# Seven products in tiles 4 to 6 and casts one tile ahead: a fused attention and feed-forward kernel on one core

## The chip, the cores and the metric

The kernel runs on one core of one Trainium2 chip. The metric is device microseconds of one execution; lower is better. TensorE (PE) multiplies, VectorE (DVE) and ScalarE (ACT) work on tiles elementwise, GpSimd (POOL) casts and issues some DMAs, SyncE (SP) issues most DMAs. All engines run their own queues and wait for each other by semaphores.

## The reference

```python
# q, k, v: (8, 8, 576, 64) float32; w_in: (512, 2048); w_out: (2048, 512)
scores = matmul(q, k^T) / sqrt(64), kept where abs(i - j) <= 32
attn   = softmax(scores)
x      = matmul(attn, v), heads side by side: (8 * 576 = 4608 tokens, 512)
h      = x @ w_in
g      = gelu_tanh(h)
out    = g @ w_out          # (4608, 512) float32
```

## The kernel before

**Tiles and batches.** The 4608 tokens are nine tiles of 512, t = 0 to 8. Tile t has a first stage, the input projection `x @ w_in` with its gelu, and a second stage, the output projection with its stores. Attention is computed per batch (b = 0 to 7, 576 tokens each) one tile ahead: tile t carries the attention of batch b = t + 1 between the products of its second stage. The result goes into `xT`, a ring of 1536 tokens from which the later tiles read.

**First stage.** `ffn_in(t, n)` makes one of 16 blocks of 128 hidden columns with four matmuls 512 wide (L577). `gelu` moves it from PSUM to `gTs[t]` on ACT (L585). After every fourth block `sums` (L694) adds and subtracts blocks on DVE into S1 to S4, four instructions for each of four groups. The first three blocks of a tile are begun at the end of the tile before (`begun`). In tiles 7 and 8 another path is taken: `in_x` (L614) makes four differences of the tokens, `in_mixed` (L632) walks the list `MIX`, and `in_product` (L616) computes two groups, A and B, of four blocks each as seven products of four matmuls 256 wide (L629) instead of 16 matmuls 512 wide. The weight sums for this come from `in_w` (L604), made earlier, in the second stages of tiles 3, 4 (group B) and 6 (group A).

**Second stage.** `ffn_out(t, i)`, i = 0 to 111, issues seven products of 16 matmuls 256 wide (L751), after the same scheme. Two PSUM banks take turns: products 0, 2, 4, 6 use one, products 1, 3, 5 the other. After each product a DVE instruction takes the bank's value (L762 to L789), and the product after the next may write to that bank only when this is done. So product 5, at i = 80, waits for L771, the DVE instruction behind product 3.

**Where attention stands.** `PLAN` says in front of which i a piece of attention is issued: "s" scores (L468) and exp (L481), "m" mask (L490, DVE), "v" sums and weighted values (L495, L505) with their inverse on ACT (L530, L531), "x" the scaled result into `xT` (L540, L546, DVE). The number is the head pair; 4 and -1 are the last 24 tokens of this and of the previous batch. `PLAN_1` is the same for tile 1.

**How the inputs come in.** At the start of tile t's second stage `load_qk(b + 1)` puts on SP's queue one DMA of 1 MB for q, four of 256 KB for k (one for each 128 keys, all heads) and the tails (the last 64 positions). At the start of the next tile, `open_and_turn` and `turn_keys` cast them to 16 bit on DVE, four instructions for q (L410) and four for k (L419); each k cast reads the same two heads of all four k DMAs. After them SP issues transposing DMAs into `QTs` and `KTs`, and `turn_tails` does the same for the tails (`KLs`). V of the next batch comes by POOL's queue at i = 4, after a copy named `after` that waits for `KLs`. SP and DVE take their queues in the program's order.

Of the kernel before, what the change touches and what calls it, by code (L numbers as in the profile page):

```python
# [36 lines left out]
def cut(b):  # L37
# [8 lines left out]
PLAN = {7: "s0@0 s1@1 v-1", 16: "m0 m1 x-1", 33: "s2@0 v0@1 v1", 36: "m2", 44: "x0", 50: "x1",  # L46
        62: "s3@0 s4@1 v2", 66: "m3", 80: "x2", 84: "m4", 91: "v3", 112: "x3"}
# [14 lines left out]
MIX = ("3 g3 A0 s0A B0 s0B 12 g12 A2 B2 cA00 cB00 A1 s1A gA00 A4 B1 s1B gB00 B4 t0 u0 13 g13 A3 s3A B3 s3B 14 g14 "  # L62
       "cA11 cB11 A5 gA10 B5 gB10 gA11 gB11 A6 B6 cA01 cB01 15 gA01 gB01 t1 t2 g15 t3 u1 u2 u3").split()
UNITS = {"A": 1, "B": 2}

PLAN_1 = {12: "s0@0 s1@1 s2", 16: "m0 m1", 36: "m2", 56: "s-1@0 v0@1 v1", 62: "m-1 x0", 64: "x1",
          78: "s3@0 v2 v-1@1", 79: "m3", 88: "x2", 91: "x-1", 97: "v3 s4@1", 112: "x3 m4"}
# [5 lines left out]

RING = 1536
# [4 lines left out]
def kernel(  # L79
# [29 lines left out]
    rawp = ctx.enter_context(tc.tile_pool(name="rawp", bufs=2))  # L109
# [27 lines left out]
    def load_early(b):  # L137


        qr = rawp.tile([128, H, 256], FP32, name="qr")  # L140
        kr = rawp.tile([128, H, 256], FP32, name="kr")
        raws[b] = [qr, kr, None]

        def qk(h0, queues=(nc.sync, nc.sync)):
            for src, dst, queue in zip((q, k), (qr, kr), queues):
                queue.dma_start(
                    dst[:, h0:h0 + 2, :],
                    src[b, h0:h0 + 2, 0:512, :].rearrange("h (p j) d -> p h (j d)", j=4))

        def vs(*cs):  # L150
            if len(raws[b]) < 4:
                raws[b].append(stage.tile([128, 4, H, 64], FP32, name="vr", tag="stage"))
                raws[b].append(tailp.tile([128, 4, 64], FP32, name="vt", tag="vt"))
            for c in cs:
                if c == 4:
                    for x in range(2):
                        nc.sync.dma_start(raws[b][4][64 * x:64 * x + 64, :, :],
                                          v[b, 4 * x:4 * x + 4, 512:S, :].rearrange("h p d -> p h d"))
                else:
                    nc.sync.dma_start(raws[b][3][:, c, :, :],  # L160
                                      v[b, :, 128 * c:128 * c + 128, :].rearrange("h p d -> p h d"))

        def tails(which="qk"):
            if raws[b][2] is None:
                raws[b][2] = tailp.tile([128, H, 64], FP32, name="tr", tag="tr")
            tr = raws[b][2]
            if b == 0:
                for i, src in enumerate((q, k)):
                    for x in range(2 if "qk"[i] in which else 0):
                        nc.sync.dma_start(tr[64 * x:64 * x + 64, 4 * i:4 * i + 4, :],  # L170
                                          src[b, 4 * x:4 * x + 4, 512:576, :].rearrange("h s d -> s h d"))
                return
            for h in (0, 4):
                for x, src in enumerate((q, k)):
                    nc.sync.dma_start(tr[64 * x:64 * x + 64, h:h + 4, :],
                                      src[b, h:h + 4, 512:576, :].rearrange("h s d -> s h d"))

        return qk, tails, vs

    def load_qk(b):  # L180


        if b == 3:
            qr = raws[3]
        else:
            qr = rawp.tile([128, H, 256], FP32, name="qr")
            load_q(b, qr)
        kr = rawp.tile([128, 4, H, 64], FP32, name="kr")
        if b > 3:
            qt = tailp.tile([16, H, 256], FP32, name="qt", tag="vt")  # L190
            kt = tailp.tile([64, H, 64], FP32, name="kt", tag="tr")
            raws[b] = (qr, kr, qt, kt)
        else:
            raws[b] = [qr, kr, tailp.tile([128, H, 64], FP32, name="tr", tag="tr"), None]
        for c in range(4):
            nc.sync.dma_start(kr[:, c, :, :],
                              k[b, :, 128 * c:128 * c + 128, :].rearrange("h p d -> p h d"))
        load_tails(b, nc.sync)
        if b == 3:
            load_vr(3)  # L200
# [4 lines left out]
    def load_tails(b, queue):  # L205
        if b > 3:
            queue.dma_start(raws[b][2], q[b, :, 512:576, :].rearrange("h (p j) d -> p h (j d)", j=4))
            queue.dma_start(raws[b][3], k[b, :, 512:576, :].rearrange("h p d -> p h d"))
        else:
            queue.dma_start(raws[b][2][0:64, :, :], q[b, :, 512:576, :].rearrange("h s d -> s h d"))  # L210
            queue.dma_start(raws[b][2][64:128, :, :], k[b, :, 512:576, :].rearrange("h s d -> s h d"))
# [190 lines left out]
    def load_vr(b):  # L402
        vr = vrs[b] = rawp.tile([128, 4, H, 64], FP32, name="qr")
        for c in range(4):
            nc.sync.dma_start(vr[:, c, :, :],
                              v[b, :, 128 * c:128 * c + 128, :].rearrange("h p d -> p h d"))

    def turn_queries(b, src, dst, p0, p1):
        for pr in range(NPAIR):
            nc.vector.tensor_copy(  # L410
                dst[:, pr, :, :, :].rearrange("p j h d -> p h j d"),
                src[:, 2 * pr:2 * pr + 2, :].rearrange("p h (j d) -> p h j d", j=4))
        nc.sync.dma_start_transpose(QTs[b].rearrange("d r j p -> d (r j) p")[:, :, p0:p1],
                                    dst.rearrange("p r j h d -> p (r j h d)"))

    def turn_keys(b):
        k16, kr = halfs[b][1], raws[b][1]
        for pr in range(NPAIR):
# [6 lines left out]
    def turn_tails(b):  # L425
        qt, kt = raws[b][2:4]
        qt16 = hp.tile([16, NPAIR, 4, 2, 64], FP16, name="qt16", tag="qt16")
        kt16 = hp.tile([64, NPAIR, 2, 64], FP16, name="kt16", tag="t16")
        turn_queries(b, qt, qt16, 128, 144)
        nc.vector.tensor_copy(kt16.rearrange("p r h d -> p (r h d)"), kt.rearrange("p h d -> p (h d)"))  # L430
        nc.sync.dma_start_transpose(
            KLs[b % 2], kt16.rearrange("p r h d -> p (r h d)"))

    def open_and_turn(b):
        cast_open(b)
        turn_queries(b, raws[b][0], halfs[b][0], 0, 128)
# [154 lines left out]
    def in_w(eng, unit, *which):  # L591
# [3 lines left out]
        if (unit, "s") not in mixed:  # L595
            halves = [(rawp if unit == "A" else yp).tile([128, 2, 2, 2, 128], FP16, name="wc" + unit + str(x),
                                                         tag=("qr", "kr")[x] if unit == "A" else "yo") for x in range(2)]
            mixed[unit, "s"] = [half[:, x] for half in halves for x in range(2)]
# [7 lines left out]
    def in_x(t):  # L606
# [3 lines left out]
        xc = hp.tile([128, 4, 2, 256], FP16, name="xc", tag="q16" if t % 2 else "k16")  # L610
# [5 lines left out]
    def in_product(unit, n):  # L616
        a, w, new = WINO[n]
        if n == 0:
            phs[unit, "a"] = psO.tile([128, 512], FP32, name="pu", tag="O") if unit == "A" else bank(1)
        elif n in (2, 4):  # L620
            which = "b" if n == 2 else "c"
            if unit == "A":
# [9 lines left out]
    def in_mixed(t):  # L632
        if "A" not in mixed:
            mixed["A"] = rawp.tile([128, 3, 512], FP32, name="sa", tag="qr")
            mixed["B"] = rawp.tile([128, 3, 512], FP32, name="sb", tag="kr")

        place = {"00": (0, "b"), "01": (1, "c"), "11": (2, "c")}
        for step in MIX:
            kind, rest = step[0], step[1:]
            if kind in UNITS:  # L640
                in_product(kind, int(rest))
# [16 lines left out]
            elif kind in "tu":  # L658
                sums(t, int(rest), slice(0, 2) if kind == "t" else slice(2, 4))
# [72 lines left out]
    def ffn_out(t, i):  # L732

        n, blk, f = i // 16, i // 8 % 2, i % 8
        if n == 1 and t >= NT - 2:
            blk, f = divmod(i % 16, 6) if i % 16 < 12 else (i // 2 % 2, 6 + i % 2)
# [28 lines left out]
        elif n == 2:  # L765
            nc.vector.tensor_copy(C11, py)
            if end:
# [162 lines left out]
    for t in range(NT):  # L930
        b = t + 1
        att = b < B
        if t:
# [8 lines left out]
            elif att:  # L942
                if b > 3:
                    open_and_turn(b)
                turn_keys(b)
                if b > 3:
                    turn_tails(b)
# [4 lines left out]
            for fc in range(begun, NF if t < NT - 2 else 0):  # L952
                ffn_in(t, fc)
                if t == 1 and fc == 3:
# [4 lines left out]
                    raws[3] = rawp.tile([128, H, 256], FP32, name="qr")  # L959
                    load_q(3, raws[3])  # L960
                    combine(4, nc.vector)
                if t == 1 and 6 <= fc < 10:
                    cast_v(2, fc - 6)
                if t == 1 and fc == 8:
                    trans_tails(1, psO.tile([128, 8, 128], FP16, name="pt", tag="O"))
# [9 lines left out]
                if t > 1 and fc == 8 and att:  # L975
                    pair_v(b, nc.vector.tensor_copy)
        plan = PLAN_0 if not t else PLAN_1 if t == 1 else PLAN if att else {40: "v-1", 66: "x-1"} if t == B - 1 else {}
# [6 lines left out]
        if t and b + 1 < B:  # L984
            load_qk(b + 1)
        ods = {}
        for i in range(113 if t else 65):
# [8 lines left out]
            for act in plan.get(i, "").split():  # L996
# [47 lines left out]
                elif kind == "m":  # L1044
                    mask(*group(g))
                elif kind == "v":
# [11 lines left out]
            if t in (3, 4) and i == 52:  # L1058
                in_w(nc.vector, "B", *((1, 2) if t == 3 else (3, 4)))
# [12 lines left out]
            elif t and i < 112:  # L1072
                ffn_out(t, i)
# [36 lines left out]
```

## Time and profile before

| | |
|---|---|
| runs | 296.6, 297.36, 1631.62 us; median 297.36 |
| profiled execution | 296.65 us |
| its span, first to last instruction | 294.6 us |
| PE busy | 285.9 us, 97% |
| DVE busy | 212.4 us, 72% |
| ACT busy | 196.5 us, 67% |
| first stage of tile 4 (176.00 to 190.38) | 14.38 us, DVE busy 11.16 |
| its second stage (190.38 to 206.50) | 16.12 us, DVE busy 11.23 |

The profile is one execution. "Span" counts from the first to the last instruction on the core; the execution's own time is 2.05 us more. The third run is far from the other two and is not used. A matmul's shown end is a model, so its start-to-start distance tells its rate: 0.216 us for 512 columns, 0.109 us for 256 columns.

### The profile page before, as it was taken

Reading aid. Unit: us, or ns where it says so; the run is one execution under the profiler, and the core shown is the slowest. Engines: PE = TensorE matmul, PEld = TensorE weight load, DVE = VectorE, ACT = ScalarE, POOL = GpSimd, SP = SyncE. Lnnn points to the kernel's source line nnn. Section 1 sums busy time; section 2 is a strip of 40 time slices with the busy share of each in tenths; the row PEclk is TensorE's granted clock in tenths of the full one; section 3 lists DMA queues with packets and bytes.
Section 4 is the critical chain, followed back from the end, with each engine's and each line's share of the span. In section 5 each row is a group of like instructions: output and inputs, shape, how many; then the busy total and the mean of one; then the engine's idle time right before and its main releaser. Section 6 shows DMA issues by size and latency. Waiting matters only on the chain.

```text
span 294.6 us, 7286 instructions
## 1 busy us (share of the span) xinstructions
PE 285.9 (97%) x2945; PEld 192.7 (65%) x2945; DVE 212.4 (72%) x467; ACT 196.5 (67%) x315; POOL 88.8 (30%) x143
## 2 busy tenths in 40 slices
PE   8889999999999999999999999999999999999993
PEld 3535545547765687568755885588558867887783
DVE  4755477998897667858796878686957877865762
ACT  5965877777677874787667776796669558706800
POOL 4445335004228713205250615050800050025000
PEclk9999999999999999999999999999999999999998
DMA  7999998999999998999999999899691040004013
GB/s 229 275 380 396 359 305 196 254 186 203 248 229 202 251 202 188 113 139 245 162 212 94 246 157 191 116 245 154 117 190 7 0 118 28 2 26 120 0 47 99
DMA packets 114392, 51.02 MB, mean 173 GB/s; under 512 B 98471, under 2 KB 110247, under 8 KB 114102
## 3 DMA queue, kind: packets, MB, share of 16 engines
q1 hardware_dynamic: 89460, 38.67, 62.4%
q0 software_dynamic: 23776, 10.83, 23.4%
q10 hardware_dynamic: 1122, 1.06, 1.1%
q8 instruction: 23, 0.38, 0.6%
q14 instruction: 11, 0.09, 0.1%
HBM read 36.70 MB, written 9.44 MB: 157 GB/s over the span
## 4 chain that ended last, share of the span: by engine, by line
PE 85%; DVE 5%; DMA 5%; issue 1%; SPq 1%; ACT 1%; POOL 0%; DVEq 0%
PE mm L751 32%; PE ph L577 17%; PE mm L577 16%; PE ps_s L468 4%; PE pu L629 3%; DMA kr<-in_k_dram 3%; PE mm L723 2%; DMA wst<-in_moe_w_in_dram 2%; PE py L723 2%; PE ps_d L495 2%; PE ps_o L505 2%; DVE t L684 2%; DVE s L694 1%; PE mm L629 1%; PE ps_od L495 1%; PE ps_od L505 1%
## 5 line engine op out<-in xcount | busy, mean ns | idle before, releaser
L577 PEld LDWEIGHTS <-w_in 128*128 128x128 f16 x512 | 57.4, 113 | 49.8 <-POOL w_in L250 1.5
L577 PE MATMUL ph<-xT,w_in 128*128 128x512 f16 x256 | 64.5, 379 | 0.6 <-POOL w_in L250 0.6
L577 PE MATMUL mm<-xT,w_in 128*128 128x512 f16 x256 | 64.1, 379 | 0.0
L585 ACT ACTIVATE gT<-mm 128x512 f16<-128x512 f32 x60 | 35.6, 598 | 33.3 <-PE mm L577 32.7
L713 POOL DMA_DIRECT2D out_dram<-y x55 | 32.8, 605 | 82.4 <-DVE y L780 75.3
L751 PEld LDWEIGHTS <-s 128*128 128x128 f16 x512 | 49.3, 98 | 7.1 <-DVE s L694 0.6
L751 PE MATMUL mm<-t,s 128*128 128x256 f16 x376 | 45.2, 273 | 0.2 <-DVE y L764 0.2
L694 DVE TENSOR_TENSOR s<-gT 128x512 f16<-128x512 f16 x64 | 27.5, 430 | 19.1 <-ACT gT L585 18.9
L751 PEld LDWEIGHTS <-gT 128*128 128x128 f16 x384 | 36.2, 98 | 6.4
L585 ACT ACTIVATE gT<-ph 128x512 f16<-128x512 f32 x58 | 32.4, 604 | 10.9 <-PE ph L577 10.9
L481 ACT ACTIVATE pe<-ps_s 128x960 f16<-128x960 f32 (+1 forms) x31 | 29.5, 975 | 13.2 <-PE ps_s L468 13.1
L751 PE MATMUL mm<-w_out,gT 128*128 128x256 f16 x256 | 32.6, 273 | 0.0
L104 ACT ACT_TABLE_LOAD x18 | 23.1, 1283 | 2.2 <-issue 1.9
L530 ACT ACTIVATE lt<-ps_d 128x480 f32<-128x480 f32 (+2 forms) x28 | 15.6, 556 | 10.4 <-PE ps_d L495 6.9
L531 ACT ACTIVATE lt<-lt 128x480 f32<-128x480 f32 (+3 forms) x36 | 21.1, 585 | 1.1
L490 DVE TENSOR_TENSOR pe<-pe,band 128x960 f16<-128x960 f16 x28 | 18.5, 680 | 2.0 <-ACT pe L481 1.9
L505 PEld LDWEIGHTS <-V 128*64 128x64 f16 x520 | 13.7, 111 | 5.5 <-DVE V L226 1.5
L751 PE MATMUL mm<-t,gT 128*128 128x256 f16 x128 | 16.1, 273 | 0.0
L694 DVE TENSOR_TENSOR s<-s,gT 128x512 f16<-128x512 f16 x32 | 14.0, 436 | 1.1
L216 POOL DMA_DIRECT2D V<-in_v_dram x16 | 14.3, 908 | 1.1 <-PE ps_s L468 0.4
L751 PE MATMUL mm<-w_out,s 128*128 128x256 f16 x120 | 14.6, 273 | 0.0
L540 DVE TENSOR_TENSOR xT<-ps_o,lt 128x480 f16<-128x480 f32 (+5 forms) x26 | 13.4, 535 | 1.6 <-PE ps_o L505 1.6
(149 smaller groups left out, 390.3 us busy)
## 6 DMA issues: line engine op xcount, KB each, us to landing
kr<-in_k_dram SPq DMA_DIRECT2D x31, 256.0 KB, 10.2
qr<-in_q_dram SPq DMA_DIRECT2D x6, 1024.0 KB, 5.9
wst<-in_moe_w_in_dram SPq DMA_DIRECT2D x8, 512.0 KB, 6.6
wst<-in_moe_w_out_dram SPq DMA_DIRECT2D x2, 1024.0 KB, 10.5
wst<-in_moe_w_out_dram SPq DMA_DIRECT2D x4, 512.0 KB, 7.4
qr<-in_v_dram SPq DMA_DIRECT2D x8, 256.0 KB, 6.5
V<-in_v_dram POOLq DMA_DIRECT2D x16, 128.0 KB, 8.5
qr<-in_q_dram SPq DMA_DIRECT2D x7, 256.0 KB, 7.3
```

Of the source, the lines that this page charges most:

```text
L104: nc.scalar.add_instruction(mybir.InstLoadActFuncSet(name=nc.get_next_instruction_name(), act_func_set_id=which, ins=[], outs=[]))
L216: nc.gpsimd.dma_start(V[:, c, :, :], v[b, :, 128 * c:128 * c + 128, :].rearrange("h p d -> p h d"))
L481: nc.scalar.activation(pe, ps[:, :, 0:w], AF.Exp, scale=SCALE)
L490: nc.vector.tensor_tensor(pe, pe, m.rearrange("k (o j) p -> k o j p", o=1).broadcast_to(list(pe.shape)), op=ALU.mult)
L505: nc.tensor.matmul(o[64 * h:64 * h + 64, cols].rearrange("d (j p) -> d j p", j=4)[:, :, p0 - q0:p1 - q0], Vs[b % 2][:, slot, 2 * pr + h, : ...
L530: nc.scalar.activation(lt[:, 0:n], d[:, 0:n], AF.Ln)
L531: nc.scalar.activation(lt[:, 0:n], lt[:, 0:n], AF.Exp, scale=-1.0)
L577: nc.tensor.matmul(ph, w_cols[:, dc, fc // 4, fc % 4, :], xT[:, dc, t * 512 % RING:t * 512 % RING + 512], start=(dc == 0), stop=(dc == 3))
L585: nc.scalar.activation(gTs[t][:, fc, :], phs[fc], AF.Gelu_apprx_tanh)
L694: nc.vector.tensor_tensor(dst, x, y, op=op)
L713: eng.dma_start(out_v[b, j, q0 + p:q0 + p + e, cols], yo[m:m + e, cols])
L751: nc.tensor.matmul(pys["apart"][:, 0:256] if apart else py[:, blk, :], lhsT, wino[w][:, f, :], start=(new and i % (8 if one else 16) == 0) ...
```

## The change

Tiles 4 to 6 (`LONE = 4` up to the last but two) go through `in_mixed` too, by a list of their own, `MIX_1`, with group B alone as seven products and the other twelve blocks as before. Their `in_x` stands at the start of the tile. The sums of w_in for group B are made in the first stage of tile 2.

The casts of q and k of batches 5, 6 and 7 move from the start of tiles 4, 5 and 6 into the second stage of tiles 3, 4 and 5: "a" and "b" in `PLAN` issue them one by one, q behind x0 and x1, k behind s3, s4 and v2, x2 and m4. Their loads move too: `load_qk(5)` stands in the first stage of tile 3, behind block 10, `load_qk(6)` and `load_qk(7)` at "load" in `MIX_1`. The tails are cast at "f0" and "f1", in the tile that uses them, and loaded there for the batch after. The tiles for raw q and k have one fixed buffer each for it (`q0`, `k0`).

`PLAN` issues most pieces of attention one to three matmuls later, `PLAN_1` too. In tile 1, `trans_tails(1)` stands behind block 6 instead of 8. In tiles 7 and 8 the sums S4 of three groups wait until behind product 2, product 1 takes its matmuls in another order, and the products A2 and B2 come before block 12.

```diff
-PLAN = {7: "s0@0 s1@1 v-1", 16: "m0 m1 x-1", 33: "s2@0 v0@1 v1", 36: "m2", 44: "x0", 50: "x1",
-        62: "s3@0 s4@1 v2", 66: "m3", 80: "x2", 84: "m4", 91: "v3", 112: "x3"}
+PLAN = {7: "s0@0 s1@1 v-1", 16: "m0 m1 x-1", 35: "s2@0 v0@1 v1", 38: "m2", 46: "x0 a0", 52: "x1 a1 a2 a3",
+        63: "s3@0 s4@1 v2 b0 b1", 67: "m3", 80: "x2 b2", 84: "m4 b3", 93: "v3", 112: "x3"}
...
-MIX = ("3 g3 A0 s0A B0 s0B 12 g12 A2 B2 ... 15 gA01 gB01 t1 t2 g15 t3 u1 u2 u3").split()
+MIX = ("3 g3 A0 s0A B0 s0B A2 B2 12 g12 ... 15 gA01 gB01 t1 t2 g15 t3 w1 w2 w3").split()
+MIX_1 = ("f0 3 B0 g3 s0B 4 B2 cB00 B1 s1B load f1 g4 5 g5 6 g6 t0 u0 B3 s3B gB00 pair B4 7 g7 cB11 gB11 12 g12 t1 u1 B5 gB10 B6 cB01 gB01 13 g13 14 g14 t2 u2 15 g15 t3 u3").split()
+PARTS = {"t": slice(0, 2), "u": slice(2, 4), "w": slice(2, 3), "z": slice(3, 4)}
...
-          78: "s3@0 v2 v-1@1", 79: "m3", 88: "x2", 91: "x-1", 97: "v3 s4@1", 112: "x3 m4"}
+          80: "s3@0 v2 v-1@1", 81: "m3", 90: "x2", 92: "x-1", 104: "v3 s4@1", 112: "x3 m4"}
...
+LONE = 4
...
-            qr = rawp.tile([128, H, 256], FP32, name="qr")
+            qr = rawp.tile([128, H, 256], FP32, name="qr", tag="q0")
             load_q(b, qr)
-        kr = rawp.tile([128, 4, H, 64], FP32, name="kr")
+        kr = rawp.tile([128, 4, H, 64], FP32, name="kr", tag="k1" if b == 3 else "k0")
...
-        load_tails(b, nc.sync)
+        if b < 6:
+            load_tails(b, nc.sync)
...
+    def turn_query(b, pr):
+        src, dst = raws[b][0], halfs[b][0]
+        nc.vector.tensor_copy(
+            dst[:, pr, :, :, :].rearrange("p j h d -> p h j d"),
+            src[:, 2 * pr:2 * pr + 2, :].rearrange("p h (j d) -> p h j d", j=4))
+        if pr == NPAIR - 1:
+            nc.sync.dma_start_transpose(QTs[b].rearrange("d r j p -> d (r j) p")[:, :, 0:128],
+                                        dst.rearrange("p r j h d -> p (r j h d)"))
...
-    def turn_keys(b):
+    def turn_keys(b, prs=range(NPAIR)):
         k16, kr = halfs[b][1], raws[b][1]
-        for pr in range(NPAIR):
+        for pr in prs:
             nc.vector.tensor_copy(k16[:, pr, :, :, :], kr[:, :, 2 * pr:2 * pr + 2, :])
...
-        for step in MIX:
+        for step in MIX if t >= NT - 2 else MIX_1:
             kind, rest = step[0], step[1:]
-            if kind in UNITS:
-                in_product(kind, int(rest))
+            if step == "pair":
+                pair_v(t + 1, nc.vector.tensor_copy)
+            elif step == "load":
+                if t + 2 < B:
+                    load_qk(t + 2)
+            elif step == "f0":
+                turn_queries(t + 1)
+            elif step == "f1":
+                turn_key_tails(t + 1)
+                if t + 2 < B:
+                    load_tails(t + 2, nc.sync)
+            elif kind in UNITS:
+                in_product(kind, int(rest), t < NT - 2)
...
-            blk, f = divmod(i % 16, 6) if i % 16 < 12 else (i // 2 % 2, 6 + i % 2)
+            blk, f = divmod(i % 16, 4) if i % 16 < 8 else (i // 2 % 2, i // 4 % 4 * 2 + i % 2)
...
             nc.vector.tensor_copy(C11, py)
+            if t >= NT - 2:
+                for step in "z1 z2 z3".split():
+                    sums(t, int(step[1]), PARTS[step[0]])
...
+                if t == 1 and fc == 6:
+                    trans_tails(1, psO.tile([128, 8, 128], FP16, name="pt", tag="O"))
                 if t == 1 and fc == 8:
-                    trans_tails(1, psO.tile([128, 8, 128], FP16, name="pt", tag="O"))
...
+                if t == 3 and fc == 10:
+                    load_qk(5)
+                if t == 2 and fc in (8, 9, 10, 11):
+                    in_w(nc.vector, "B", (8, 9, 10, 11).index(fc) + 1)
-        plan = PLAN_0 if not t else PLAN_1 if t == 1 else PLAN if att else {40: "v-1", 66: "x-1"} if t == B - 1 else {}
+        plan = PLAN_0 if not t else PLAN_1 if t == 1 else PLAN if att else {16: "v-1", 40: "x-1"} if t == B - 1 else {}
...
-        if t and b + 1 < B:
+        if t in (1, 2):
             load_qk(b + 1)
...
+                elif kind in "ab":
+                    if 2 < t < B - 2:
+                        if kind + str(g) == "a0":
+                            cast_open(b + 1)
+                        turn_query(b + 1, g) if kind == "a" else turn_keys(b + 1, (g,))
...
-            if t in (3, 4) and i == 52:
-                in_w(nc.vector, "B", *((1, 2) if t == 3 else (3, 4)))
```

## The prediction

> **What bounds the kernel now.** I read the page's head first, then the busy time by stage.
>
> ```profile
> span 294.6 us, 7286 instructions
> PE 285.9 (97%) x2945; PEld 192.7 (65%) x2945; DVE 212.4 (72%) x467; ACT 196.5 (67%) x315; POOL 88.8 (30%) x143
> DMA  7999998999999998999999999899691040004013
> ```
> ```profile
> core 0: us, PE busy (x) PEld busy (x) DVE busy (x) ACT busy (x) POOL busy (x), PEclk, DMA share, GB/s
> 145.50:159.90 14.40, 14.40 (x72) 7.77 (x70) 11.27 (x30) 9.13 (x16) 6.19 (x10) 1.00 1.07 151
> 159.90:176.00 16.10, 16.10 (x264) 13.26 (x262) 12.49 (x26) 12.50 (x18) 5.07 (x7) 1.00 1.39 199
> 190.38:206.50 16.12, 16.12 (x265) 13.35 (x263) 11.23 (x20) 12.52 (x18) 4.70 (x7) 1.00 1.30 185
> ```
>
> PE is never free in tiles 2 to 6, so only less PE work makes them shorter. The DMA row matters as much: the DMA engines are 90% busy until about 220 us. PE's pace hides them, but what must land earlier than now has no idle DMA time to come from. The stages above are those of tile 3 (first and second) and tile 4's second. Next, SP's queue in tile 3's second stage, which starts at 159.9 (columns: start, duration), and the time from issue to landing of the k loads, in this window and in the whole run.
>
> ```profile
> 159.66 1.20 SPq L431 DMA_TRANSPOSE KL<-kt  x1
> 160.91 0.58 SPq L203 DMA_DIRECT2D qr<-in_q_dram  x1
> 161.54 6.04 SPq L196 DMA_DIRECT2D kr<-in_k_dram  x4
> 167.63 3.42 SPq L207 DMA_DIRECT2D qt<-in_q_dram  x1
> ```
> ```profile
> DMA to landing us min/median/max: 9.4/9.4/9.4
> ```
> ```profile
> DMA to landing us min/median/max: 5.6/10.2/12.7
> ```
>
> Batch 5's loads follow batch 4's transposes, which keep SP from 148.4 to 160.9. The fourth k load is issued at 166.54. With the median of 10.2 us it lands at 176.7, and the trace's last semaphore update for it stands at 177.0. Today the first of the four k casts starts at 178.66, and product 3's L771 stands in DVE's queue long before it:
>
> ```profile
> 168.96 0.68 DVE L604 TENSOR_TENSOR wcB<-w_in 128x512 f16<-128x512 f16 x1
> 169.56 0.68 DVE L604 TENSOR_TENSOR wcB<-w_in,wcB 128x512 f16<-128x512 f16 x1
> 170.63 0.69 DVE L771 TENSOR_TENSOR y<-mm,y 128x512 f32<-128x512 f32 x1 [0.39 <-PE mm L751]
> 178.66 1.42 DVE L419 CAST k<-kr 128x512 f16<-128x512 f32 x4
> ```
> ```profile
> 172.18 1.04 PE L751 MATMUL mm<-t,gT 128*128 128x256 f16 x8
> ```
>
> The last row is product 5 of tile 3 at i = 80, which waits for L771.
>
> **The change part by part.**
>
> *Seven products.* In the chain of waits, 8 matmuls of 512 columns take 1.73 us (0.216 each) and 16 of L629 take 1.75 (0.109 each). Per tile, 16 x 0.216 = 3.46 becomes 28 x 0.109 = 3.06: 0.39 saved, 1.17 in tiles 4 to 6. DVE in their first stages loses eight casts (1.46 + 1.42) and gets four differences (a step of 0.34 each in tile 7: 1.4) and one copy with three additions (a step of 0.6: 2.4). That is 0.9 more beside some 11 of 14 us. ACT gets two copies of 0.59 beside 9.1. Both have room; if they had none, the gelus would be late by these sums. Blocks 4 to 15 keep at least a block's time between gelu and bank reuse when I lay out `MIX_1` by these durations, so I expect no new PE wait there.
>
> *The weight sums* (2.4 at L604's step) go to tile 2's first stage. DVE waits for gelus there about 3 us per tile (the 1.90, 0.62 and 0.62 shown ahead of L694 in the next tiles), which cover them. Without that, tile 2's last sums would be up to 2.4 late, which product 1's 1.1 us of slack at its last blocks would not hide.
>
> *Tile 1.* The second group of tail transposes starts 0.53 late (65.80, where 64.41 + 4 x 0.216 gives 65.27), for L360 behind four sums. Moved two blocks up, it is free: 0.53 gained at most, nothing at least.
>
> *Tiles 7 and 8.* The chain shows DVE's sums ahead of the y that PE needs:
>
> ```profile
> 280.83 1.34 DVE s L694 x4
> 282.17 0.61 DVE y L764
> 282.83 2.78 PE mm L751 x24
> ```
>
> Product 2 starts at 280.74 and takes 16 x 0.109 = 1.75, so product 3 starts 0.34 late. Three sums fewer ahead of L764 (3 x 0.34) remove this. Product 1 takes 1.95 in both tiles, 0.20 above 1.75; it waits for the second group's sums, which the new order asks for later. Together 0.34 + 0.20 + 0.20 = 0.74, at least nothing.
>
> *Attention's pieces later.* Two matmuls are 0.22 us. Pieces and their readers move together, so nothing waits for it. The price is in DVE's order in tiles 4 and 5: x0, a0, y (L766), x1, a1 to a3, b0, b1, then L771. From tile 4's rows (x0 at 197.58), L771 ends at about 202.4 instead of 201.8; product 5 starts at 202.66. That is 0.3 us to spare; without it, each us late is one on PE.
>
> *The casts one tile ahead.* In tiles 4 and 5 the load stands about 5 us behind the start of the first stage, the cast of k 24 us behind it. Issue to last landing takes 16.1 to 16.9 us (160.91 to 177.0 here), so some 3 us remain. Behind it on SP stand the transposes for `KL`, so V's load on POOL, behind `after`, may start 2 us later than now; its first reader, `pair_v`, comes 20 us later.
>
> Tile 3 is different. `load_qk(5)` stands in its first stage, but on SP it is still behind the transposes of batch 4, so it goes out at 160.9 as now. q lands 5.8 us later (166.7), and a0 comes at 168: in time. b0 comes at 170.5 and needs all four k loads: 177.0. DVE takes its queue in order, so behind b0 wait L771, m3, L774, x2. PE goes on to i = 79 and stands at i = 80: b0 and b1 0.68, L771 0.69, so product 5 starts at about 178.45 instead of 172.18. That is **6.3 us lost**. The bounds are the shortest and the longest landing of a k load, 5.6 and 12.7: 1.4 and 8.5. I take 6.3, which is from the very DMA.
>
> *The clock behind the stall.* The granted clock is halved after PE stands still:
>
> ```profile
> 290.00:292.80 2.80, 0.00 (x0) 0.00 (x0) 0.42 (x1) 0.00 (x0) 0.00 (x0) 1.00 0.64 170
> 292.90:294.60 1.70, 0.00 (x0) 0.00 (x0) 0.00 (x0) 0.00 (x0) 0.00 (x0) 0.50 0.00 0
> ```
>
> The last matmul ends at 290.0, and at 292.9 the clock is at 0.50. A pause of 6 us is twice that. At the start the spin matmuls of 512 columns come each 0.43 us from 1.26 to about 6.2, 4.9 us, before they come each 0.22. No pause inside the run shows the return: its bounds are 0 and 4.9 / 2 = 2.5 us lost. I take 3.9 us at half clock, between the 2.9 of the fall and the 4.9 of the rise: **2.0 lost**.
>
> [...]
>
> *Sum.* Gains 1.17 + 0.74, and half of tile 1's 0.53, since the stall's end is set by the DMAs and not by PE: 2.2. Loss 6.3 + 2.0 = 8.3. The span becomes 294.6 - 2.2 + 8.3 = 300.7. Around it lie 2.05 us in the profiled execution (296.65): **302.7 us**. That is 2.0% above that execution and 1.8% above the median of 297.36.
>
> **Rivals.**
>
> *No stall (0.06).* If the keys land before 170.5, the change is faster: 294.6 - 2.4 + 2.05 = 294.2. For it speaks only that the load's call stands earlier. Against it: even the shortest k landing, 5.6 us after 166.54, is 172.1, and SP has nothing free before 160.9.
>
> *Stall with a full clock (0.16).* The pause costs 6.3 and no more: 300.7. For it speaks that no row shows the clock inside a run; against it, that 2.9 us were enough at the end.
>
> *Tiles 4 and 5 stall too (0.16).* If their k loads take over 19 us from issue to landing, b0 is late there as well. The stores of the tile before (eight DMAs, 1 MB) would run beside these loads; today they run beside transposes. From 24.1 us behind the first stage's start on, each us counts; at 2 us in each tile it is 306.7, with more half clock up to 310. Against it speaks that V's load now starts behind most of k's.
>
> *The main case (0.62)* is one stall in tile 3 with a half clock behind it, 301.3 to 304.2.
>
> **How the numbers follow.** "Faster" and "slower" mean by over 2%, about what a measurement of this kernel can tell from no change. The limit, 302.6 over the profiled execution, lies in the middle of the main case: 0.62 gives 0.31 slower and 0.31 same. The full clock adds 0.16 same, the stall in three tiles 0.16 slower, no stall 0.05 same and 0.01 faster; together faster 0.01, same 0.52, slower 0.47. The range holds the main case, the full clock and the lower half of the third rival: 298.6 to 306.3. Left out are no stall and its worst, some 0.15.
>
> **What would show it.** In the profile after, DVE's first k cast in tile 3's second stage waits for the kr DMA by 5.5 to 7 us, PE pauses about 6 us ahead of i = 80, once, and the clock is at 0.5 for 3 to 5 us behind it. Tiles 4 to 6 take 30.0 us instead of 30.4, product 3 of tile 8 starts without a gap. The prediction is wrong if PE has no pause there, if the pause is under 4 us, or if tiles 4 and 5 have one too.

## The result, and the profile after

| | before | after |
|---|---|---|
| runs, median | 297.9 us (6 runs) | 305.56 us (302.9 to 309.4, 6 runs) |
| after to before | | 1.0263, 95% interval 1.0221 to 1.0304: slower |
| profiled execution, its span | 296.65, 294.6 us | 305.99, 304.0 us |

The six runs before include the one of 1631.62 us; without it their median is 297.36. The ratio is taken from fast runs alone, so it is not quite the quotient of the medians. Predicted were 302.7 us in a range of 298.6 to 306.3.

The tile numbers have to be set right first. In the prediction's readings between 145.5 and 206.5 us, and in the last rows of the table on the profile before, each stretch is called one tile too low; tiles 1, 7 and 8 are named rightly. The window 145.50 to 176.00 is tile 4, not 3, and 176.00 to 206.50 is tile 5, so the loads read there are those of batches 6 and 7. Below, tiles are counted by the first L591 (input projection) and the first L781 (output projection) of each; L751, L771 and L419 of the kernel before are L781, L804 and L434 now.

The page of the changed kernel, its head and the granted clock in 40 slices:

```profile
span 304.0 us, 7400 instructions
...
PE 287.4 (95%) x2981; PEld 197.5 (65%) x2981; DVE 222.8 (73%) x491; ACT 196.5 (65%) x321; POOL 86.9 (29%) x143
...
PEclk9979999999999999999679999999999999999999
```

PE's busy time hardly changes (half-speed matmuls make up for the saved ones), its share falls from 97 to 95%, and the clock dips twice: in the third slice, which belongs to the start-up, and in the middle. By stage (same columns as before), tile 3's second stage and tile 4's first:

```profile
130.28:157.70 27.42, 19.23 (x268) 14.90 (x267) 13.80 (x28) 12.91 (x18) 5.37 (x8) 0.81 1.12 166
157.70:171.11 13.41, 13.41 (x78) 8.31 (x77) 11.22 (x27) 8.64 (x17) 4.76 (x9) 1.00 0.76 199
```

In the kernel before, tile 3's second stage took 16.61 us and tile 4's first 13.81. So one stage loses 10.81 us, and the stage with seven products gains 0.40. What happens inside, on SP's queue, on DVE, on PE, and in the chain that ended last (columns: start, duration, what):

```profile
131.72 1.20 SPq L444 DMA_TRANSPOSE KL<-kt  x1
132.98 0.57 SPq L205 DMA_DIRECT2D qr<-in_q_dram  x1
133.61 7.70 SPq L197 DMA_DIRECT2D kr<-in_k_dram  x4
```

```profile
149.73 0.76 DVE L434 CAST k<-kr 128x512 f16<-128x512 f32 x2 [8.01 <-DMA kr<-in_k_dram]
150.41 0.69 DVE L804 TENSOR_TENSOR y<-mm,y 128x512 f32<-128x512 f32 x1
```
```profile
141.94 1.47 PE L781 MATMUL mm<-t,s 128*128 128x256 f16 x12
151.15 2.93 PE L781 MATMUL mm<-t,gT 128*128 128x256 f16 x13 [7.73 <-DVE y L804]
```
```profile
135.70 3.12 SPq L197
...
138.87 10.64 DMA kr<-in_k_dram
```

The loads of batch 5 go out directly behind the last transpose of batch 4. DVE's copy b0 waits 8.01 us for the last k DMA of batch 5, issued at 138.87 and landed at 149.51. L804, queued behind it, comes at 150.41, and product 5 (i = 80) starts at 151.15. The last matmul of product 4 had ended at 143.25: a pause of 7.9 us. The clock around it, by windows:

```profile
146.10:151.10 5.00, 0.00 (x0) 0.00 (x0) 1.37 (x4) 0.00 (x0) 0.00 (x0) 0.50 1.32 156
151.20:156.30 5.10, 5.10 (x36) 3.30 (x36) 3.25 (x7) 1.59 (x3) 0.00 (x0) 0.50 0.66 129
156.40:157.70 1.30, 1.30 (x15) 1.17 (x13) 0.66 (x2) 0.77 (x1) 0.91 (x2) 1.00 0.04 8
```

It halves at 146.10, 2.9 us after PE stopped, and stays at 0.50 for 5.2 us after PE has work again (0.213 us for 256 columns instead of 0.109).

Stage by stage, the two profiled executions differ by +9.4 us: tile 3's second stage +10.81; the first stages of tiles 4, 5 and 6 -0.40, -0.39, -0.41; tiles 7, 8 and the tail behind them -1.21; tile 1 -0.53 and -0.24; tile 2's first stage +0.51; the start-up +1.23; the rest within 0.04. "Start-up" is the time to the first matmul of tile 0's output projection (L723 before, L753 after). In the profile after, PE waits 1.19 us there for V's cast on GpSimd, which waits for its DMA, and the clock is at half from 16.40 to 19.81; neither shows in a profile of the kernel before. The medians, which do not hang on one execution, differ by 7.7 us.

### The profile page after: what moved, and what is told of

Its sections match the earlier page's. It is cut to its first block, busy times and chain, and to the rows that moved or that the text cites. A ratio compares the mean times of both kernels' runs of the same rounds, so it can differ in the third digit from the quotient of the medians.

```text
span 304.0 us, 7400 instructions
## 1 busy us (share of the span) xinstructions
PE 287.4 (95%) x2981; PEld 197.5 (65%) x2981; DVE 222.8 (73%) x491; ACT 196.5 (65%) x321; POOL 86.9 (29%) x143
## 4 chain that ended last, share of the span: by engine, by line
PE 81%; DMA 9%; SPq 5%; POOL 2%; DVE 1%; issue 1%; ACT 1%; ACTq 0%; DVEq 0%; POOLq 0%
PE mm L781 29%; PE ph L591 16%; PE mm L591 13%; PE pu L647 6%; DMA vr<-in_v_dram 4%; DMA kr<-in_k_dram 4%; PE ps_s L482 3%; PE py L753 2%; PE mm L753 2%; PE ps_d L509 2%; PE ps_o L519 2%; SPq L197 2%; DMA qr<-in_q_dram 1%; SPq L409 1%; PE mm L647 1%; POOL out_dram L743 1%
## 5 line engine op out<-in xcount | busy, mean ns | idle before, releaser
L591 PEld LDWEIGHTS <-w_in 128*128 128x128 f16 x464 | 52.2, 114 | 41.6 <-issue 0.8
L591 PE MATMUL ph<-xT,w_in 128*128 128x512 f16 x244 | 61.6, 381 | 0.0
L591 PE MATMUL mm<-xT,w_in 128*128 128x512 f16 x220 | 56.5, 380 | 0.0
L743 POOL DMA_DIRECT2D out_dram<-y x55 | 30.5, 564 | 87.9 <-DVE y L813 81.5
L781 PEld LDWEIGHTS <-s 128*128 128x128 f16 x512 | 49.7, 98 | 6.4
L781 PEld LDWEIGHTS <-gT 128*128 128x128 f16 x384 | 36.8, 99 | 15.0 <-issue 7.9
L781 PE MATMUL mm<-t,s 128*128 128x256 f16 x376 | 44.9, 273 | 0.0
L599 ACT ACTIVATE gT<-mm 128x512 f16<-128x512 f32 x36 | 21.3, 599 | 27.6 <-PE mm L591 27.2
L781 PE MATMUL mm<-w_out,gT 128*128 128x256 f16 x256 | 32.6, 273 | 0.0
L599 ACT ACTIVATE gT<-ph 128x512 f16<-128x512 f32 x43 | 23.8, 606 | 8.6 <-PE ph L591 8.6
L781 PE MATMUL mm<-t,gT 128*128 128x256 f16 x128 | 17.8, 291 | 7.7 <-DVE y L804 7.7
L519 PEld LDWEIGHTS <-V 128*64 128x64 f16 x520 | 14.4, 114 | 6.5 <-POOL V L877 1.3
L434 DVE CAST k<-kr 128x512 f16<-128x512 f32 x24 | 9.1, 419 | 8.5 <-DMA kr<-in_k_dram 8.5
L781 PE MATMUL mm<-w_out,s 128*128 128x256 f16 x120 | 15.0, 277 | 0.0
```

The costliest lines, as they stand in the source:

```text
L519: nc.tensor.matmul(o[64 * h:64 * h + 64, cols].rearrange("d (j p) -> d j p", j=4)[:, :, p0 - q0:p1 - q0], Vs[b % 2][:, slot, 2 * pr + h, : ...
L591: nc.tensor.matmul(ph, w_cols[:, dc, fc // 4, fc % 4, :], xT[:, dc, t * 512 % RING:t * 512 % RING + 512], start=(dc == 0), stop=(dc == 3))
L599: nc.scalar.activation(gTs[t][:, fc, :], phs[fc], AF.Gelu_apprx_tanh)
L743: eng.dma_start(out_v[b, j, q0 + p:q0 + p + e, cols], yo[m:m + e, cols])
L781: nc.tensor.matmul(pys["apart"][:, 0:256] if apart else py[:, blk, :], lhsT, wino[w][:, f, :], start=(new and i % (8 if one else 16) == 0) ...
```

## The experiments

The theory: one pause in tile 3, because b0 there needs a k DMA that SP issues behind batch 4's transposes, and a half clock behind it; everything else in the change gains a little. Rivals: the pause belongs to the seven products or to something that only tile 3 has; the gains aren't there; the half clock costs nothing. The edits are to the changed kernel.

### The copies of batch 5's keys moved to the end of tile 3

```diff
-                    if 2 < t < B - 2:
+                    if 2 < t < B - 2 and not (t == 3 and kind == "b"):
...
+            if t == 3 and i == 112:
+                turn_keys(5)
```

> The kernel after, with the four k casts of batch 5 (and with them the transposes behind them) moved from i = 63, 80 and 84 to i = 112 of tile 3, behind x3. Theory: DVE's queue order makes the stall; the wait for k moves to the tile's end, where k lands some 2.6 us late. Behind it stand the last sums of tile 3's output, the token differences of tile 4 and the copy that its product 1 needs, so PE stands about 3 us early in tile 4 and the clock stays mostly full: about 298. Rival, that the keys' lateness costs the same wherever it is waited for: one pause of about 8 us again, 305.6.

Measured: 297.23 us, ratio 0.9975 (0.9936 to 1.0013). No pause ahead of product 5, full clock from 4.7 us to the last matmul, tile 3's second stage 16.59 us. The wait is still there, only at the end, and PE feels it in tile 4 (DVE, then PE):

```profile
150.35 1.43 DVE L434 CAST k<-kr 128x512 f16<-128x512 f32 x4 [2.83 <-DMA kr<-in_k_dram]
```
```profile
155.90 0.60 PE L647 MATMUL pu<-xw 128*128 128x256 f16 x4 [1.93 <-DVE sb L674]
```

With another 0.6 there, tile 4's first stage takes 16.31 us, 2.9 over the changed kernel's. So 8.3 us of the changed kernel's time hang on where four copies stand in one tile: the theory's place is right.

### The V load of batch 5 held back

The first form put `load_v(5)` later in the program (i = 64 instead of 4), alone and with the copies at the end.

```diff
-            if t > 1 and i == 4 and b + 1 < B:
+            if t > 1 and i == (64 if t == 3 else 4) and b + 1 < B:
```

> The kernel after, with the load of V for batch 5 (POOL's queue) in front of i = 64 of tile 3's second stage instead of i = 4. Theory: the stall ends with the landing of the fourth k DMA of batch 5, and that DMA shares the DMA engines with V. In tiles 4 and 5 of the profile after, where V starts behind most of k, q's issue to k's last landing takes 12.9 and 11.4 us, against 16.5 in tile 3. So k lands about 4 us sooner, PE stands 3 to 4 us instead of 7.9 in front of product 5, and the time falls by 4 us (about 301.5), by 6 (299.5) if the clock stays full. Rival, that SP's issues and not the shared DMA engines set the landing: it stays at 16.5 us, and the time at 305.6.

> Both edits: V of batch 5 at i = 64, and the four k casts of batch 5 at i = 112. Theory: k lands about 145 and the casts stand at about 146.5, so nobody waits for it, PE has no pause, the clock stays full, and what is left are the gains: 305.6 - 7.9 - 2.6 = about 295, under 1% below the kernel before. Rival, that the early casts load DVE too much in tiles 3 to 5 whatever the keys do: pauses of PE in front of product 5 in tiles 4 and 5, and a time above the kernel before.

Measured: 306.21 us (1.0273, 1.0216 to 1.0331), and 298.42 us (0.998, 0.9939 to 1.002). Neither tested anything new: GpSimd's queue waits for no matmul between i = 4 and 64, so in the first V went out from 136.0 us on, 1.7 us behind q's issue as in the changed kernel, k landed 16.8 us behind q's issue, and the pause was 7.8 us. The second only repeats the copies at the end (k at 17.1 us, PE's waits 0.6 and 1.9 us again). The next form made the load wait for data:

```diff
-                nc.gpsimd.tensor_copy(after, KLs[b % 2][:, 3, 0:1])
+                nc.gpsimd.tensor_copy(after, wino["yo"][:, 2, 256:257] if t == 3 else KLs[b % 2][:, 3, 0:1])
```

> In tile 3 alone, the one-column copy on GpSimd in front of batch 5's V load reads what VectorE writes behind product 4 (i = 63) instead of a key tail, so that the V load leaves GpSimd's queue at about 140 us instead of 136, behind all of the q and k DMAs (133.0 to 138.9 us in the changed kernel). Theory (q, k and V of batch 5 share the DMA engines, so V's 1 MB holds back k's last DMA): the last k DMA lands 3 to 4 us earlier, at 12 to 13 us behind q's issue as in tiles 4 and 5 (12.9 and 11.4) instead of 16.5; the pause falls from 7.9 to 4 to 5 us and the time from 305.6 to about 302. Rival (the k DMAs are late because SyncE's queue hands them out late, and V costs them nothing): landing, pause and time unchanged, 305.6.

Measured: 302.36 us, 1.0117 (1.0068 to 1.0166). The last k DMA landed at 145.55, 12.5 us behind q's issue at 133.07, instead of 16.5. SP's queue, GpSimd's, and PE's list of waits:

```profile
133.07 0.58 SPq L205 DMA_DIRECT2D qr<-in_q_dram  x1
133.71 7.66 SPq L197 DMA_DIRECT2D kr<-in_k_dram  x4
```
```profile
147.75 2.68 POOL L220 DMA_DIRECT2D V<-in_v_dram  x3
```
```profile
PE mm L781 <- DVE y L804: 3.0, 1, 3.0
```

The half clock around the pause lasted 3.4 us. SP handed out the k loads as in the changed kernel (7.66 us against 7.70), and they still landed 4 us earlier. So V's load on GpSimd's queue costs k's loads on SyncE's 4 us. In the two later profiles with V held back the last k landed 12.8 us behind q's issue, in all others, with V beside it, 16.5 to 17.8. V went out even later than planned (147.75 us), since what it waits for is the held-up L804 itself. So the rival that V costs k nothing falls. That the other part is SP's late issue is read from its queue; no run took the loads out from behind the transposes.

### The pause without its half clock

Matmuls that nothing reads were to fill the pause. In the first form they used the buffer that batch 5's transposes write to, and so waited themselves:

```diff
+                if t == 3 and i == 80:
+                    spin(34, 512, psO.tile([128, 512], FP32, name="spin", tag="D"))
```

> The kernel after, with 34 matmuls of 512 columns into an unused PSUM bank in front of product 5 of tile 3, so that PE works (7.3 us) while DVE waits for the keys. Nothing else differs. Theory: in the profile after, the clock is at 0.5 for 10.2 us around the pause, 5.2 us of it after PE is back, which costs 2.6 us; with PE busy the clock stays full and the time falls by about 2.6, to 303. Rival, that behind the pause PE is held by DVE's queue and not by its clock: no change, 305.6.

Measured: 314.83 us (1.0573, 1.0518 to 1.0627), with a pause of 10.1 us in front of the added matmuls. It tells nothing of the clock. In the second form the operands were the identity and `w_in16`:

```diff
+                if t == 3 and i == 80:
+                    warm = psO.tile([128, 512], FP32, name="warm", tag="D")
+                    for _ in range(34):
+                        nc.tensor.matmul(warm, idn, w_in16[:, 0, 0:512], start=True, stop=True)
```

> 34 products of 512 columns that nothing reads, on operands that have long been ready (the 128x128 identity and the input weights), are issued in tile 3 just ahead of product 5; they fill TensorE for 34 x 0.213 = 7.2 us of the 7.9 us in which it stands still in the changed kernel, and delay nothing that VectorE waits for. Theory (the pause itself costs 7.9 us, and the half clock behind it another 2.6 us): the clock stays at 1.0 across the pause, the 256-column matmuls behind it take 0.109 us instead of 0.213, and the time falls from 305.6 by about 2.6 to 303.0 us. Rival (the half clock is only what the profile prints; the matmuls behind the pause are slow because they wait for something else): no change from 305.6. Should the copy of batch 5's keys come earlier in this run, the added products would themselves set the end, at about the same time.

Measured: 306.6 us (1.0252, 1.0182 to 1.0323; the four runs 303.8 to 307.8). The time does not show the 2.6 us. The profiled execution does, by stage: its first L781 came 3.5 us later than in the changed kernel's profile, and k landed 20.0 us behind the stage's start instead of 19.2, but the stage took 25.77 us instead of 27.42. From product 5's start to the stage's end it is 4.17 us (155.33 to 159.50) against 6.55 (151.15 to 157.70):

```profile
155.40:159.50 4.10, 4.10 (x48) 3.42 (x48) 3.91 (x8) 2.17 (x3) 0.46 (x1) 1.00 0.44 86
```

That is 2.4 us for the half clock, shown by the rows of two executions and not by the times.

### The whole step one tile later

```diff
-LONE = 4
+LONE = 5
...
-                if t == 3 and fc == 10:
-                    load_qk(5)
+                if t == 4 and fc == 10:
+                    load_qk(6)
...
-                    if 2 < t < B - 2:
+                    if 3 < t < B - 2:
```

(with the casts and loads of the tiles before moved along in the same way)

> The changed kernel with all that begins in tile 3 and 4 moved one tile on: seven products in tiles 5 and 6 alone, casts one tile ahead from batch 6. Theory (the pause belongs to the first tile whose second stage holds the casts ahead, because q and k are loaded there only behind the transposes of the batch before): tile 3 has no pause, and one of 6 to 8 us stands in tile 4 in front of product 5 (i = 80): 6.3 by the profile before of tile 4's loads (issue 160.5, landing 177.0), with half clock behind it. Time: the changed kernel's 305.6, plus 0.4 for the gain of seven products in one tile given up, less up to 1.6 for the earlier landing: 304 to 306 us. Rival (the pause is tile 3's own, from the one-time casts of batch 4 in its first stage): no pause in tile 4, 296 to 298 us.

Measured: 305.31 us, 1.0224 (1.016 to 1.0288). Tile 3's second stage took 16.59 us, tile 4's 25.66. SP's queue and DVE in tile 4:

```profile
161.46 8.07 SPq L197 DMA_DIRECT2D kr<-in_k_dram  x4
```
```profile
177.97 0.76 DVE L434 CAST k<-kr 128x512 f16<-128x512 f32 x2 [6.40 <-DMA kr<-in_k_dram]
```

The pause goes with the first tile of the new order, and in tile 4 PE waits 6.4 us, where the prediction had worked out 6.3 from that tile's rows. The rival of a cause peculiar to tile 3 falls.

### Each half of the change alone

Without casts ahead, `MIX_1` has B0 behind block 5, `open_and_turn`, `turn_keys` and the tails stand ahead of `in_x` again, and the loads are where they were:

```diff
-                    if 2 < t < B - 2:
+                    if False:
...
-                if t == 3 and fc == 10:
-                    load_qk(5)
...
-        if t in (1, 2):
+        if t and b + 1 < B:
             load_qk(b + 1)
```

> The changed kernel without casts ahead: the casts of every batch stand again at the start of its tile, loads at the start of the second stage, the mixing of the group's inputs behind them; seven products in tiles 4 to 6, tiles 1, 7 and 8 as in the changed kernel. Theory (the seven products gain 0.4 us a tile, with tiles 1, 7 and 8 about 3.1 us in all, and only the casts ahead lose): no pause in tile 3, and the time is 297.9 - 3.1 = 294.8 us if VectorE gets through casts, mixing and copies within the first stage. Rival (without casts ahead VectorE has no room in tiles 4 to 6: 12 casts and 8 mixing operations ahead of the first mixed product): TensorE waits 1 to 5 us in the first stage of each of the three tiles, and the time is 298 to 310 us.

Without seven products, `MIX_1` holds the blocks 3 to 15 as ordinary products, and `in_x` is left out in tiles 4 to 6:

```diff
-MIX_1 = ("f0 3 B0 g3 s0B 4 B2 cB00 B1 s1B load f1 g4 5 g5 ... 15 g15 t3 u3").split()
+MIX_1 = "f0 3 g3 t0 u0 4 g4 5 g5 load f1 6 g6 7 g7 t1 u1 pair 8 g8 ... 15 g15 t3 u3".split()
...
-                if t >= LONE:
-                    in_x(t)
-                elif t > 1:
+                if 1 < t < LONE:
```

> The other half of the pair with the seven products alone: casts, loads and V's pairing one tile ahead as in the changed kernel, but tiles 4 to 6 compute all 16 column blocks as ordinary products (no mixing of inputs, no seven products). Theory (the pause belongs to the casts ahead alone; seven products gain 0.4 us in each of three tiles): the pause of 7 to 8 us in front of product 5 of tile 3 with half clock behind it stays, first stages of tiles 4 to 6 take 13.8 us again, and the time is 305.6 + 1.2 = 306.8 us. Rival (the pause needs the seven products too, by the copies and buffers that they take): no pause, about 297 us.

| | casts ahead | casts at the tile's start |
|---|---|---|
| seven products | 305.56 us; first stages of tiles 4 to 6: 13.41, 13.42, 13.41; pause in tile 3 | 297.81 us (0.9989, 0.9953 to 1.0025); 13.99, 14.09, 13.93; no pause |
| ordinary products | 308.2 us (1.0297, 1.0243 to 1.035); 13.82, 13.82, 13.82; pause 8.2 us | before: 297.9 us; 13.81, 13.81, 13.82; no pause |

The pause is the casts' alone. The 0.4 us a tile needs both halves, as far as this one order of `MIX_1` without casts ahead can tell: with the casts at the tile's start, DVE is busy for 13.17 of the 13.99 us of tile 4's first stage (first row), and PE waits for it (second row, from its list of waits):

```profile
145.62:159.61 13.99, 13.60 (x79) 8.27 (x78) 13.17 (x33) 8.79 (x17) 6.15 (x10) 1.00 0.96 162
```
```profile
PE pu L646 <- DVE sb L673: 1.2, 3, 0.5
```

Here the rival held in its kind (DVE has no room) but not in its size: 0.6 us a tile over the changed kernel, not 1 to 5.

### Both edits together, and the kernel before once more

> Both edits that worked, in tile 3 alone: batch 5's V load waits on GpSimd for what VectorE writes behind product 4, and the four copies of batch 5's keys stand at the end of the stage (i = 112) instead of i = 63 to 84. Theory: the last k DMA lands some 12.5 us behind q's issue (measured with the V load late) instead of 16.5 to 17, that is before i = 112, so the 2.8 us that VectorE waited there, and the 0.6 + 1.9 us that TensorE then waited in tile 4, are gone; what is left of the changed kernel are its gains of about 3.1 us less the 0.5 us at tile 3's first scores: 297.9 - 2.6 = 295.3 us, ratio 0.990 to 0.993. Rival (the late V load is itself late in tile 4, or the four copies, 1.4 us, hold back the last sum of tile 3 and with it tile 4's first mixed products): 297 to 298 us, as with the copies at the end alone.

> The kernel with the late V load and the key copies at the end of tile 3, profiled a second time beside the kernel before. Theory (the stages of tiles 3 to 8 are what the two edits make of them, and only start-up and tile 2 scatter): second stage of tile 3 16.6 to 17.5 us, first stages of tiles 4 to 6 13.41 us each, no wait of VectorE for k, full clock throughout tiles 3 to 8, and with the start-up of 15.3 us, as before had it, a span of about 293 us. Rival (the gain shown by its ratio of 0.993 was chance): 297 us or more with full clock and the same start-up.

> The kernel before, unchanged, profiled a second time. Eight of nine profiles of the changed kernel and its variants have a first stage of tile 2 between 14.7 and 18.1 us (the other 14.05) with a wait of TensorE for GpSimd's cast t of the tail (0.5 to 2.6 us), the one profile of before 14.15 and no such wait; their start-up lies between 14.8 and 19.1 us. Theory (both scatter from run to run and are no part of the change): this profile differs from the first one of the same kernel by 0.3 us or more in start-up or in tile 2's first stage. Rival (the wait in tile 2 comes with the change): again 14.1 to 14.2 us, no wait.

Measured for the late V load with the key copies at i = 112: 296.78 us, 0.9929 (0.9899 to 0.9959), and in a second set of runs 296.81 us, 0.9977 (0.9943 to 1.0012). Its second profile has a span of 294.0 us, full clock throughout, and the copies without a wait:

```profile
146.55 1.42 DVE L434 CAST k<-kr 128x512 f16<-128x512 f32 x4
```

It beats the changed kernel by nearly 9 us. Against the kernel before its two ratios are 0.2 and 0.7% below 1, one with its interval below 1 and one across it, so that a gain there is not settled; 295.3 us were expected. Some of the gain goes back: its second stages of tiles 3 to 5 take 16.96, 16.87 and 17.20 us where before took 16.6 to 16.7. Why was not tried.

The kernel before, profiled again (median 297.14 us), has the same 14.15 us in tile 2's first stage and no wait there. Of the twelve profiles of the changed kernel and its variants ten have 14.66 us or more (the expectation had left out one of the two without, 14.04 and 14.05). That speaks for the rival, a wait of some 0.5 us that comes with the change, and is not proof. The start-up is the same in both profiles of before too (its end at 32.69 and 32.84 us); in the twelve others it ends between 32.5 and 37.4, six of them at 33.0 or less. The six longer ones have a wait of PE for V of 1.0 to 1.5 us in it, and in five of these the clock is at half for 3.4 or 6.8 us with it; the six short ones have neither, so it is no fixed cost of the change. Whether the change makes it more frequent stays open.

## Why the prediction was right in kind and 3 us short

| step | predicted, us | measured in the profiled pair, us |
|---|---|---|
| seven products, tiles 4 to 6 | -1.17 | -1.20 |
| sums and order of tiles 7 and 8 | -0.74 | -1.21 |
| tile 1 | -0.26 (half of 0.53) | -0.77 |
| weight sums to tile 2 | 0 | +0.51 |
| scores of tile 3 | not foreseen | +0.53 |
| the pause in tile 3 | +6.3 | +7.9 |
| half clock behind it | +2.0 | +2.4 |
| start-up | 0 | +1.23 |

*The pause: mechanism right, size off.* The step that failed is the size of this term, 6.3 where 7.9 was measured. The name was right (tile 3, i = 80, b0, L804 behind it, once) and so was the way it was worked out, but the rows were those of tile 4, through the wrong label. In the kernel before, SP's queue in the true tile 3 reads:

```profile
131.23 0.58 SPq L203 DMA_DIRECT2D qr<-in_q_dram  x1
131.86 6.10 SPq L196 DMA_DIRECT2D kr<-in_k_dram  x4
```

Its last k DMA landed at 148.09, 18.8 us behind that stage's start at 129.32; in tile 4 the same was 17.3 (159.74 to 177.0). The same sum from these rows gives 6.3 + 1.5 = 7.8. The run with everything one tile later, 6.4 us in tile 4, also says that the label was the error and the method wasn't. Agreement to 0.1 us is partly luck: in the second profile of before the two landings come 19.5 and 16.2 us behind their stages' starts. And the prediction named only SP's order as what makes k late; 4 us of the 16.5 were V's load.

*The half clock.* Predicted 3.9 us at half clock behind the pause, measured 5.2. Two readings at the ends of the run bounded it (2.9 by the granted clock; 4.9 by the pace of the first matmuls, where the record of the clock already reads 1.00, so that this one is an estimate) and the measured value lies above both. In the variants the clock was at half around the pause for 3.4, 6.8, 6.8 and 6.8 us, for pauses of 3.2, 6.5, 7.8 and 8.2 us (V held back by data, the step one tile later, V's call moved, ordinary products), and for 10.2 us here with 7.9. In the four variants 3.4, 5.0, 2.6 and 3.3 us of it lay behind the pause, so 3.9 is within what the executions scatter.

*Gains.* The seven products brought what was counted, 0.4 a tile. That DVE "has room" for them was true only with the casts ahead. The edits of tiles 7 and 8 brought 0.47 more than the gap that the chain showed: tile 7's stages became shorter as well (-0.14, -0.30). Tile 1's first stage gained its 0.53 in full, in every profile (14.26 against 14.79 and 14.80); the further 0.24 in its second stage lies within what that stage scatters in the variants (16.76 to 17.27).

No run takes the edits of tiles 1, 7 and 8 out by themselves; that the gains are theirs is read from stages that come out alike in all twelve profiles with them (14.26 in tile 1's first; 13.18 and 12.79 in tile 7).

*Costed at nothing.* The weight sums raise DVE's time in tile 2's first stage from 10.34 to 12.54 us. DVE covered them, as argued; but PE's transposes there wait 0.45 us for GpSimd's cast of the tails. It took 0.85 us instead of 0.62 and began 0.28 us later, 11.79 us into the stage. The longer time goes with the weight sums: in eleven profiles the cast runs beside one or two of them and takes 0.81 to 1.16 us, in the one where it doesn't 0.65. Alone it is not enough for a wait: in the two profiles without one the cast took 0.96 us but began at 11.0 to 11.1. The weight sums were not moved to try it. In tile 3 the first scores wait 0.5 us for batch 4's transposes of k; the step left those out. Such a wait shows in three of the twelve profiles (0.46, 0.57 and 2.30 us), so it is no fixed cost either.

*The sum.* The costs came out 4.3 us above what was counted and the gains 1.0 us, so part of the error is hidden by luck. The start-up's 1.23 is this execution's and was in no step.

*The rivals.* "No stall" and "full clock" fall by the rows above. "Tiles 4 and 5 stall too" falls: from q's issue to the last k landing it is 12.9 and 11.4 us there (162.66 to 175.54, 192.79 to 204.22), less than the 16.1 to 16.9 assumed, and PE has no pause. That their V load starts behind k was argued then; in tile 3, holding V back gave the same 12.5. The limit of 2% lay in the middle of the main case, and the missing 3 us put the result on its far side: 305.56 lies above the main case's 301.3 to 304.2, and "same", at 0.52 the likelier verdict, did not come. Of the signs given, VectorE's wait (8.0 us, said 5.5 to 7) and the half clock behind the pause (5.2, said 3 to 5) lay above; tiles 4 to 6 took 30.0 to 30.1 us, as said.

## What to carry to other kernels

When work is moved one stage ahead, look first at the one stage where the old order still feeds the new: its loads stand where they stood, behind the old queue, while their reader has come forward. Name the stage by its own first instruction before taking durations from it, since neighbours that do the same work differed here by 1.5 us in when the same DMA landed, and by 3.3 in a second profile. And a saving on one engine may rest on room that another part of the same change makes: run each half alone.

## What the runs showed of the hardware that was not expected

A load on GpSimd's queue, issued between SyncE's, delayed SyncE's last 256 KB by 4 us (16.5 to 17.8 against 12.5 to 12.8 us from q's issue). Moving its call 60 matmuls later in the program moved it by nothing (1.7 us behind q's issue both times); only a data dependence did (14.7 us). A pause of 3.2 us was enough for 3.4 us of half clock, and the loss depended on more than the pause's length: 7.8 to 8.2 us led to 6.8 us of it in two executions, and 7.9 us to 10.2 in a third. It also came behind two short waits: in the start-up of the profile after, 1.19 and 0.39 us were followed by 3.4 us at half clock, while 1.53 and 0.39 us at the same place were followed by none in the profile with the copies at the end.

GpSimd's cast of the tails took 0.81 to 1.16 us in the eleven profiles where weight sums ran on VectorE beside it, and 0.62 to 0.65 in the three where none did. That the one causes the other was not tried.
